# Sliding-window attention and an ELU layer on one core: other ways to build the constants, and loads of q, k, v cut in halves

## The chip, the core and the metric

The kernel runs on one core of a Trainium2 chip. A core has five engines that run their own instruction streams and wait for each other by semaphores: TensorE (PE in the profile; PEld is its weight load), VectorE (DVE), ScalarE (ACT), GpSimd (POOL) and SyncE (SP, which here only issues transfers). Data lie in an on-chip memory of 128 partitions; PE writes into accumulation banks (PSUM). Transfers are run by 16 DMA engines and are issued here from SP or from POOL. The metric is the device time of one execution in microseconds (us), lower is better; the time of a kernel is the median over its runs.

## What is computed

Attention over 8 batches and 8 heads, 576 positions of 64 values, with a causal window of 128 and a linear bias by distance, and then a layer with ELU on the result. Cut to what matters:

```python
scores = q @ k^T / sqrt(64)
rel = pos[:, None] - pos[None, :]
slopes = 2.0 ** (-8.0 * (arange(8) + 1) / 8)
scores = where((rel >= 0) & (rel < 128), scores - slopes * abs(rel), -1e9)
attn = softmax(scores) @ v                        # 8 x 8 x 576 x 64
x = attn.transpose(0, 2, 1, 3).reshape(4608, 512)
h = x @ w_in                                      # 512 -> 2048
out = where(h > 0, h, exp(min(h, 0)) - 1) @ w_out # 2048 -> 512
```

All inputs and the output are float32; the kernel works in float16 with float32 accumulation.

## The kernel before

**One list of slots.** Work is put into numbered slots by `at(slot, function, ...)` (L541); the loop at the end (L655) walks the slots and emits, in each: scores, one group of 16 or 8 `hidden` matmuls, `elu` of the group before, the attention work, then everything else in the order in which it was registered, and one group of `output` matmuls. The order within each engine is therefore the order written here; only semaphores move work in time. A slot takes about 2.1 us once all parts run. From the first `hidden` groups one reads where slots lie: slot 4 at 18.7 us, 8 at 25.0, 9 at 26.5, 10 at 28.2, 11 at 29.9, 13 at 33.9, 14 at 36.4, 18 at 46.1, 21 at 53.9, 25 at 68.4.

**Attention.** Each batch has 16 score groups (`BANKS`), one per slot, that start at slot 16b + 5 for batch b from 1 on. `scores` (L350) multiplies 32-position-ordered blocks of k and q out of `QK[b % 2]`, a tile of 128 partitions x 5 blocks x (q, k) x 8 heads x 128. Partitions 0 to 63 hold the transposed q and k. For batch 0 only these are used, and the bias comes from a second matmul with `DM` and `cI` (L378). From batch 1 on the partitions from 64 on carry constants, so that one matmul gives scores, bias and part of the mask: 32 rows of group flags (64 to 95; `g_`) and in 96 to 127 (`r_`) two rows for the bias, the others being zero. ACT takes the exponential (`EX`, L382), DVE cuts it with `band` (`cut`, L390), PE multiplies with v (`values`, L404), DVE normalizes into `xn` (L424, L425), and `turn` brings it as columns into `xT`: by PE for batches 0 and 1, by a transposing DMA on SP (L433) from batch 2 on.

**The layer.** `hidden` (L452): PE into `hp` (three banks), ACT exponential `e` (L465), POOL clamps `e` (L466). `elu`: DVE makes `g` from `e` and `hp` (L473), which also frees the bank. `output` (L492) follows some 10 slots later. From group 40 on there are four slots between the `turn` that completes 256 columns of `xT` and the `hidden` that reads them.

**Inputs.** q and k go by POOL-issued DMAs, with a cast, into `stq[b]` (512 positions, `load_qk`, L78) and `stt[b]` (the last 64, `load_tail`), v into `vs[b]` (`load_v4`) and its tail straight into `VP[b % 2]`. Each of these tiles has two buffers. DVE transposes q and k in 32x32 blocks into `tt` (`squares`, L327) and SP copies them into `QK` (`collect`, L333), eight of each per batch; batch 1 goes through PE (`transposes`). `place_v` (L116) moves 32 partitions of v at a time into `VP`, mostly on POOL: 16 pieces per batch. For batches 3 to 7 the code loads b + 2 during batch b: k at s0 + 10, q at s0 + 13, v at s0 + 15, tails at s0 + 26 and + 27, v's tail at s0 + 19, and v's pieces two per slot from s0 + 20 to s0 + 27, where s0 = 16b + 5.

**Constants.** `posi`, an int32 iota of positions (L154), is written on POOL in the preamble. `groups`, `flags`, `terms` and `group_rows` (L227 to L259) work it into `TQ` and `TK` on DVE in slots 9 to 13; `fill_q` (ACT) and `fill_k` (POOL) spread these over the heads into `QK[1]` in slots 14 to 26, `k_term` (DVE, eight times, slots 14 to 19) writes the bias rows, one per head, and `fill_other` (SP, slots 21 to 28) copies the 64 constant partitions of `QK[1]` to `QK[0]`, block by block. `last_blocks` (DVE, slot 12) makes the last 128 columns of `DM`, `bands` makes `band` from it, and `zeros` (DVE, slot 4) clears padding.

Of the kernel before, what the change touches and what calls it, by code (L numbers as in the profile page):

```python
# [19 lines left out]
def kernel(  # L20
# [33 lines left out]
    def one(shape, dt, name):  # L54
        return const.tile(shape, dt, name=name, tag=name)
# [47 lines left out]
        nc.gpsimd.dma_start(  # L103
            stt[b][:, w, :, :], (q, k)[w][b, :, 512:576, :].rearrange("h s d -> s h d"))

    def load_v4(b):

        vs[b] = stage.tile([128, H, 4, D], F16, name="vs", tag="vs", bufs=2)
        nc.gpsimd.dma_start(vs[b].rearrange("p h j d -> p h (j d)"),
                            v[b, :, 0:512, :].rearrange("h (p j) d -> p h (j d)", j=4))  # L110

    def load_v4_tail(b):
        nc.gpsimd.dma_start(VP[b % 2][0:64, 4, :, 0:D],
# [24 lines left out]
    with tc.manual_schedule():  # L138

        row = one([128, 1], I32, "row")  # L140
        col = one([128, 128], I32, "col")
        posi = one([128, 576], I32, "posi")
        load_half(0, 1, 0, 0, 4)
        load_half(0, 0, 0, 0, 4)
        nc.gpsimd.iota(row, pattern=[[0, 1]], base=0, channel_multiplier=1)
# [5 lines left out]
        load_half(0, 1, 1)  # L151
        load_half(0, 0, 1)
        load_v_half(0, 1)
        nc.gpsimd.iota(posi[:, 0:512].rearrange("p (n j i) -> p n j i", j=4, i=32),  # L154
                       pattern=[[128, 4], [1, 4], [4, 32]], base=0, channel_multiplier=0)
        nc.gpsimd.iota(posi[:, 512:576], pattern=[[1, 64]], base=512, channel_multiplier=0)

        def small(name, dt=F32):
            return one([128, 1], dt, name)
# [16 lines left out]
        def seen(c, t, key, off, n):  # L176

            V.tensor_scalar(out=nd[:, c:c + n], in0=t, scalar1=key, scalar2=-1.0,
                            op0=ALU.subtract, op1=ALU.mult)
            if off:  # L180
                V.tensor_scalar(out=nd[:, c:c + n], in0=nd[:, c:c + n], scalar1=float(-off),
                                scalar2=None, op0=ALU.add)
# [15 lines left out]
        unseen(128, 128, -127.0, ALU.is_lt)  # L198
        join(0, 256)

        def last_blocks():
            seen(256, posi[:, 512:576], kpos, -384, 64)
            seen(320, posi[:, 512:576], rowf, -512, 64)
            unseen(256, 64, -127.0, ALU.is_lt)
            unseen(320, 64, 0.0, ALU.is_gt)
            join(256, 128)

        def bands():
            V.tensor_scalar(out=band, in0=DM, scalar1=-1000.0, scalar2=BIG, op0=ALU.is_gt, op1=ALU.mult)

        def zeros():
            for i in range(2):
                V.memset(QK[i][0:64 + 64 * i, 4, 1, :, 64:128], 0.0)
                V.memset(VP[i][64:128, 4, :, 0:D], 0.0)
            for e in EX:
                V.memset(e[:, 512:576], 0.0)


        g_, r_ = slice(64, 96), slice(96, 128)
        gof = small("gof")  # L220
        is96, is97, isx = small("is96"), small("is97"), small("isx")
        TQ = one([128, 640], F16, "TQ")
        TK = one([128, 640], F16, "TK")
        gi = one([128, 320], I32, "gi")
        pm = one([128, 576], F32, "pm")

        def groups():  # L227
            V.tensor_scalar(out=gof, in0=rowf, scalar1=-8.0, scalar2=1024.0, op0=ALU.mult, op1=ALU.add)
            V.tensor_scalar(out=gi[g_, 0:256], in0=posi[g_, 0:256], scalar1=gof[g_, :], scalar2=None,
                            op0=ALU.add)  # L230
            V.tensor_scalar(out=gi[g_, 256:320], in0=posi[g_, 512:576], scalar1=gof[g_, :],
                            scalar2=None, op0=ALU.add)
            V.tensor_scalar(out=gi[g_, :], in0=gi[g_, :], scalar1=255, scalar2=None,
                            op0=ALU.bitwise_and)

        def flags():
            V.tensor_scalar(out=is96, in0=rowf, scalar1=96.0, scalar2=None, op0=ALU.is_equal)
            V.tensor_scalar(out=is97, in0=rowf, scalar1=97.0, scalar2=None, op0=ALU.is_equal)
            V.tensor_scalar(out=isx, in0=is97, scalar1=-1.0, scalar2=None, op0=ALU.mult)

        def terms():

            flags()
            V.tensor_scalar(out=pm[r_, :], in0=posi[r_, :], scalar1=float(-MID), scalar2=None, op0=ALU.add)
            V.tensor_scalar(out=TQ[r_, 0:576], in0=pm[r_, :], scalar1=isx[r_, :], scalar2=is96[r_, :],
                            op0=ALU.mult, op1=ALU.add)
            V.tensor_scalar(out=TK[r_, 0:576], in0=pm[r_, :], scalar1=is96[r_, :],
                            scalar2=is97[r_, :], op0=ALU.mult, op1=ALU.add)
            for t in (TQ, TK):
                nc.gpsimd.memset(t[64:128, 576:640], 0.0)  # L250

        def group_rows():
            for d0, s0, n in ((0, 0, 256), (512, 256, 64)):
                V.tensor_scalar(out=TQ[g_, d0:d0 + n], in0=gi[g_, s0:s0 + n], scalar1=134.5,
                                scalar2=-30000.0, op0=ALU.is_gt, op1=ALU.mult)
                V.tensor_scalar(out=TK[g_, d0:d0 + n], in0=gi[g_, s0:s0 + n], scalar1=7.5,
                                scalar2=None, op0=ALU.is_lt)
            for t in (TQ, TK):
                V.tensor_copy(t[g_, 256:512], t[g_, 0:256])  # L259

        def fill_q(n):
            nc.scalar.copy(QK[1][64:128, n, 0, :, :],
                           TQ[64:128, 128 * n:128 * n + 128].unsqueeze(1).broadcast_to([64, H, 128]))

        def fill_k(n):
            nc.gpsimd.tensor_scalar(  # L266
                out=QK[1][g_, n, 1, :, :], in0=TK[g_, 128 * n:128 * n + 128].unsqueeze(1)
                .broadcast_to([32, H, 128]), scalar1=1.0, scalar2=0.0, op0=ALU.mult, op1=ALU.add)

        def k_term(h):  # L270
            V.tensor_scalar(out=QK[1][r_, :, 1, h, :], in0=TK[r_, :].rearrange("p (n c) -> p n c", c=128),
                            scalar1=8.0 * 2.0 ** (-8.0 * (h + 1) / H), scalar2=None, op0=ALU.mult)

        def fill_other(n):
            nc.sync.dma_start(QK[0][64:128, n].rearrange("p w h c -> p (w h c)"),
                              QK[1][64:128, n].rearrange("p w h c -> p (w h c)"))

# [70 lines left out]
        def scores(b, s):  # L350
            i, p = BANKS[s]
            t = ps_s.tile([128, 512], F32, name="sp", tag="sps")
            qk = QK[b % 2]

            r = 64 if b == 0 else 128

            def mm(o, h, kc, qc, n):
                nc.tensor.matmul(t[:, o:o + n], qk[0:r, kc, 1, h, :], qk[0:r, qc, 0, h, 0:n],  # L358
                                 start=b > 0 or o == 0, stop=b > 0)

            if i == 0:
                hs = [4 * p + l for l in range(4)]
                for l in range(4):
                    mm(128 * l, hs[l], 0, 0, 128)
            elif i < 4:
                hs = [2 * p, 2 * p + 1]
                for l in range(2):
                    mm(256 * l, hs[l], i, i, 128)
                    mm(256 * l + 128, hs[l], i - 1, i, 128)
            else:  # L370
                hs = [4 * p + l for l in range(4)]
                for l in range(4):
                    mm(128 * l, hs[l], 3, 4, 64)
                    mm(128 * l + 64, hs[l], 4, 4, 64)
            if b == 0:
                c, n = columns(i)
                for l, h in enumerate(hs):
                    nc.tensor.matmul(t[:, n * l:n * l + n], cI[:, h, :], DM[:, c:c + n],  # L378
                                     start=False, stop=l == len(hs) - 1)
            e = ex[b, s] = EX[count[0] % 4]  # L380
            count[0] += 1
            nc.scalar.activation(e[:, 0:512], t, AF.Exp, scale=0.125)  # L382
# [189 lines left out]
        for b in range(B):  # L572
# [25 lines left out]
                    at(s0 + (6 + n if b > 1 else 8 + n if n < 4 else 9 + n), collect, b + 1, n)  # L598
                at(s0 + (24 if b else 31), transposes_tail, b + 1)
            if b + 2 < B and b:  # L600
                for i, w in enumerate((1, 0)):
                    at(s0 + 10 + 3 * i, load_qk, b + 2, w)
                    at(s0 + 26 + i, load_tail, b + 2, w)
                at(s0 + 15, load_v4, b + 2)
                at(s0 + 19, load_v4_tail, b + 2)
                for n in range(4):
                    for u in range(2):
                        at(s0 + 20 + 2 * n + u, place_v, b + 2, n, (2 * u, 2 * u + 1), nc.gpsimd)


        at(6, place_v, 0, 2, (0, 1), nc.gpsimd)
        at(7, place_v, 0, 2, (2,), nc.gpsimd)
        at(7, place_v, 0, 2, (3,), nc.scalar)
        for u in range(2):
            at(10 + u, place_v, 0, 3, (2 * u, 2 * u + 1), nc.gpsimd)
        at(3, load_wi, 3)
        at(5, load_wo, 0, 1)
        at(8, load_wo, 1, 1)
        at(9, load_wo, 2, 1)
        at(10, load_wo, 3, 1)  # L620
        at(4, zeros)
        at(9, groups)
        at(10, terms)
        at(12, last_blocks)
        at(13, group_rows)
        at(14, bands)
        for n, m in enumerate((14, 16, 18, 23, 26)):
            at(m, fill_q, n)
            at(m, fill_k, n)
        for h in range(H):  # L630
            at(14 + 3 * h // 4, k_term, h)
        for n in range(5):
            at((21, 22, 23, 25, 28)[n], fill_other, n)
        for i, w in enumerate((1, 0)):
# [69 lines left out]
```

## Time and profile before

| | |
|---|---|
| median of 11 runs | 352.06 us (349.36 to 354.47) |
| the profiled execution | 351.41 us |
| its span | 349.6 us |
| granted PE clock, mean | 0.99 |
| busy: PE, DVE, POOL, ACT | 327.9, 249.5, 212.7, 208.0 us |
| DMA issued by POOL (q, k, v, weights) | 18.35 MB |
| DMA issued by SP and others (output, collect, transposes, copies) | 20.46 MB |
| landing: full load of q, k or v, 512 KB | 8.1 to 8.9 us, median |
| landing: collect, QK<-tt, 128 KB | 2.4 us |
| landing: transpose, xT<-xn | 3.6 us |
| landing: fill_other, QK<-QK, 256 KB | 2.9 us |

The span is the part of the execution between the first and last instruction; 1.8 us lie around it. Busy time of an engine is the time in its instructions, and PE's is modelled, so that a full PE is not a PE at its peak. In the lines of a timeline the columns are start, duration, engine, source line, operation, result and operand with their shapes, number of instructions merged, and in brackets the idle time in front and what ended it. Transfers are listed with their time from issue to landing.

### The profile page before, as it was taken

What the parts mean: (1) busy time and instruction counts of PE and PEld (TensorE: products, weight loads), DVE (VectorE), ACT (ScalarE), POOL (GpSimd) and SP (SyncE); (2) the same over time, 40 slices, a digit from 0 to 9 for tenths busy, and PEclk for the clock granted to TensorE, in tenths of its full rate; (3) what the DMA queues carried; (4) which work ended last, traced back from release to release, by engine and by line L of the source; (5) the groups of instructions that cost most, each with busy time, mean ns of one, the idle gap of its engine ahead of it and who ended that gap; (6) DMA issues with size and microseconds to landing.
All of it is one profiled execution on the core that took longest, in us unless ns stands there. A gap on an engine that the chain in (4) does not pass through costs nothing.

```text
span 349.6 us, 9328 instructions
## 1 busy us (share of the span) xinstructions
PE 327.9 (94%) x3604; PEld 242.7 (69%) x3604; DVE 249.5 (71%) x572; ACT 208.0 (59%) x360; POOL 212.7 (61%) x325
## 2 busy tenths in 40 slices
PE   5899996798999969999999999999999999999995
PEld 4678674577777747877777777777777777666663
DVE  4468986888779678958994999498967676533330
ACT  5566658676885636665666666666566656344431
POOL 8538994454788945896589568957972223333330
PEclk9699999999999999999999999999999999999999
DMA  7998999647893797569947974896462222311122
GB/s 90 179 203 119 184 177 181 125 84 123 126 169 79 110 191 107 98 105 194 122 107 120 191 106 99 141 193 93 104 108 54 55 47 52 68 35 30 32 60 61
DMA packets 66428, 39.54 MB, mean 113 GB/s; under 512 B 31120, under 2 KB 60048, under 8 KB 66384
## 3 DMA queue, kind: packets, MB, share of 16 engines
q0 software_dynamic: 41936, 18.35, 44.5%
q1 hardware_dynamic: 24272, 20.46, 26.4%
q8 instruction: 28, 0.46, 0.6%
q14 instruction: 16, 0.13, 0.1%
q10 hardware_dynamic: 176, 0.13, 0.1%
HBM read 36.70 MB, written 9.44 MB: 132 GB/s over the span
## 4 chain that ended last, share of the span: by engine, by line
PE 74%; POOL 8%; DVE 6%; DMA 5%; ACT 3%; issue 2%; SPq 1%; POOLq 0%; ACTq 0%; DVEq 0%
PE hp L461 30%; PE op L504 29%; PE sp L358 7%; PE av L404 4%; DMA xT<-xn 3%; POOL VP L121 3%; POOL e L466 2%; DMA QK<-tt 2%; PE spare L536 2%; DVE g L473 1%; ACT EX L382 1%; PE sp L378 1%; DVE QK L296 1%; DVE xn L425 1%; POOL QK L266 1%
## 5 line engine op out<-in xcount | busy, mean ns | idle before, releaser
L466 POOL TENSOR_SCALAR e<-e 128x512 f32<-128x512 f32 x144 | 90.4, 629 | 116.4 <-ACT e L465 101.6
L461 PE MATMUL hp<-xT,wi 128*128 128x256 f16 (+3 forms) x1536 | 150.2, 246 | 3.3 <-DMA xT<-xn 1.7
L473 DVE SCALAR_TENSOR_TENSOR g<-e,hp 128x512 f16<-128x512 f32 x144 | 98.0, 681 | 66.8 <-POOL e L466 65.8
L504 PE MATMUL op<-wo,g 128*128 128x512 f16 x560 | 143.1, 379 | 0.0
L461 PEld LDWEIGHTS <-wi 128*128 128x128 f16 x1536 | 117.8, 98 | 17.8 <-issue 3.7
L465 ACT ACTIVATE e<-hp 128x512 f32<-128x512 f32 x144 | 86.1, 598 | 48.2 <-PE hp L461 47.1
L382 ACT ACTIVATE EX<-sp 128x512 f16<-128x512 f32 x128 | 76.5, 598 | 63.1 <-PE sp L358 52.5
L121 POOL TENSOR_SCALAR VP<-vs 32x512 f16<-32x512 f16 x105 | 69.1, 659 | 8.1 <-DMA vs<-in_v_dram 1.1
L504 PEld LDWEIGHTS <-g 128*128 128x128 f16 x560 | 47.1, 97 | 34.3
L358 PEld LDWEIGHTS <-QK 128*128 128x128 f16 (+1 forms) x576 | 39.1, 98 | 30.5 <-issue 3.7
L390 DVE TENSOR_TENSOR EX<-EX,band 128x512 f16<-128x512 f16 x112 | 54.8, 489 | 4.8 <-ACT EX L382 4.1
L358 PE MATMUL sp<-QK 128*128 128x128 f16 (+3 forms) x576 | 50.3, 215 | 3.0 <-ACT EX L382 1.4
L404 PE MATMUL av<-VP,EX 128*128 128x65 f16 x576 | 38.8, 194 | 4.8 <-DVE EX L390 1.9
L404 PEld LDWEIGHTS <-EX 128*128 128x128 f16 x576 | 32.1, 98 | 7.9 <-DVE EX L390 2.4
L425 DVE TENSOR_TENSOR xn<-av,rden 128x256 f16<-128x256 f32 x80 | 34.0, 425 | 2.8
L327 DVE STREAM_TRANSPOSE tt<-stq 128x512 f16<-128x512 f16 x48 | 33.6, 701 | 1.5 <-DMA QK<-tt 1.5
L508 ACT COPY ob<-op 128x512 f32<-128x512 f32 x35 | 20.5, 587 | 15.6 <-PE op L504 15.1
L424 DVE RECIPROCAL rden<-av 128x4 f32<-128x4 f32 x80 | 14.0, 176 | 5.9 <-PE av L404 5.7
L536 PE MATMUL spare<-ident 128*128 128x128 f16 x84 | 9.0, 277 | 3.8 <-DVE kmod L169 3.8
L125 ACT COPY VP<-vs 32x512 f16<-32x512 f16 x17 | 10.5, 615 | 0.4
L536 PEld LDWEIGHTS <-ident 128*128 128x128 f16 x84 | 7.2, 128 | 4.0 <-DVE kmod L169 3.8
L346 DVE COPY QK<-tpt 64x512 f16<-64x512 f16 x16 | 6.7, 418 | 0.5 <-PE tpt L341 0.4
(85 smaller groups left out, 146.3 us busy)
## 6 DMA issues: line engine op xcount, KB each, us to landing
out_dram<-ob SPq DMA_DIRECT2D x126, 64.0 KB, 1.9
QK<-tt SPq DMA_DIRECT2D x48, 128.0 KB, 2.4
stq<-in_k_dram POOLq DMA_DIRECT2D x7, 512.0 KB, 8.1
stq<-in_q_dram POOLq DMA_DIRECT2D x7, 512.0 KB, 8.3
vs<-in_v_dram POOLq DMA_DIRECT2D x7, 512.0 KB, 8.9
wi<-in_moe_w_in_dram POOLq DMA_DIRECT2D x4, 512.0 KB, 9.8
wo<-in_moe_w_out_dram POOLq DMA_DIRECT2D x4, 512.0 KB, 7.4
QK<-QK SPq DMA_DIRECT2D x5, 256.0 KB, 2.9
```

Source lines behind the costliest of these rows:

```text
L121: engine.tensor_scalar(out=o, in0=i, scalar1=1.0, scalar2=0.0, op0=ALU.mult, op1=ALU.add)
L327: V.transpose(out=tt[b][:, dh, w, hs, :, :].rearrange("p h j i -> p (h j) i"), in_=stq[b][:, w, hs, :, 32 * dh:32 * dh + 32].rearrange("p ...
L358: nc.tensor.matmul(t[:, o:o + n], qk[0:r, kc, 1, h, :], qk[0:r, qc, 0, h, 0:n], start=b > 0 or o == 0, stop=b > 0)
L382: nc.scalar.activation(e[:, 0:512], t, AF.Exp, scale=0.125)
L390: V.tensor_tensor(out=e, in0=e, in1=band[:, c:c + n].unsqueeze(1).broadcast_to([128, 512 // n, n]), op=ALU.min)
L404: nc.tensor.matmul(a[:, l, :], e[:, c:c + 128], vp[:, n, h, 0:D + 1], start=st, stop=sp)
L425: V.tensor_tensor(out=xnt[b, i][:, 4 * half:4 * half + 4, :], in0=a[:, :, 0:D], in1=r.unsqueeze(2).broadcast_to([128, 4, D]), op=ALU.mult)
L461: nc.tensor.matmul(p[:, l * w + u0:l * w + u1], w_in_sb[:, c, fc * 128:(fc + 1) * 128], xT[:, c, x0:x0 + u1 - u0], start=(c == 0), stop=(c ...
L465: nc.scalar.activation(e, p, AF.Exp)
L466: nc.gpsimd.tensor_scalar(out=e, in0=e, scalar1=1.0, scalar2=0.0, op0=ALU.min, op1=ALU.max)
L473: V.scalar_tensor_tensor(out=gs[t][:, f0:f0 + nf, c0:c0 + w], in0=sh(es.pop((t, j))), scalar=1.0, in1=sh(hps.pop((t, j))), op0=ALU.subtrac ...
L504: nc.tensor.matmul(ops[t], gs[t][:, fc, ts * 128:(ts + 1) * 128], w_out_sb[:, fc, :], start=(fc == 0), stop=(fc == NFC - 1))
```

## The change

The constants are built by other means. Two rows of positions (`kterm` on eight partitions, `qterm` on one) come from iotas on POOL as float32 and float16; the slopes by head come from an iota over the exponent bits; ones, and the slopes as rows, from memsets on DVE (`tables`). One DVE operation makes the eight bias rows (`terms`). Ten small DMAs on SP (`spread`, slot 11) put them into partitions 96 and 97 of `QK[1]` and 97 of `TQ`; `k_term`, `flags` and `group_rows` are gone. The group flags come from an iota that already counts groups. The constants now end at partition 97: `scores` uses 98 rows, and `fill_q` and `fill_other` handle 34 partitions. `last_blocks` uses an iota and a copy of columns that `DM` already has. `zeros` has one memset more.

The loads of q, k and v of batches 3 to 7 are each cut in two by heads (0 to 3 and 4 to 7). With o = s0 + 2, + 4 and + 1 for b = 1, b = 2 and b from 3 on, the k halves are at o and o + 2, q at o + 4 and o + 6, v at o + 8 and o + 10, the tails at o + 12 and o + 14; v's tail stays. v's pieces are placed one per slot from s0 + 18 to s0 + 33. Of batch 0's fourth v block, the pieces that were in slots 10 and 11 are in 9 and 10, and one goes to DVE.

```diff
@@ -103,11 +103,12 @@
         nc.gpsimd.dma_start(
             stt[b][:, w, :, :], (q, k)[w][b, :, 512:576, :].rearrange("h s d -> s h d"))
 
-    def load_v4(b):
-
-        vs[b] = stage.tile([128, H, 4, D], F16, name="vs", tag="vs", bufs=2)
-        nc.gpsimd.dma_start(vs[b].rearrange("p h j d -> p h (j d)"),
-                            v[b, :, 0:512, :].rearrange("h (p j) d -> p h (j d)", j=4))
+    def load_v4(b, h0=0, h1=H):
+
+        if b not in vs:
+            vs[b] = stage.tile([128, H, 4, D], F16, name="vs", tag="vs", bufs=2)
+        nc.gpsimd.dma_start(vs[b][:, h0:h1, :, :].rearrange("p h j d -> p h (j d)"),
+                            v[b, h0:h1, 0:512, :].rearrange("h (p j) d -> p h (j d)", j=4))
 
     def load_v4_tail(b):
         nc.gpsimd.dma_start(VP[b % 2][0:64, 4, :, 0:D],
@@ -139,7 +140,11 @@
 
         row = one([128, 1], I32, "row")
         col = one([128, 128], I32, "col")
-        posi = one([128, 576], I32, "posi")
+
+        gi = one([128, 320], I32, "gi")
+        slope = one([H, 1], I32, "slope")
+        kterm = one([H, 640], F32, "kterm")
+        qterm = one([1, 640], F16, "qterm")
         load_half(0, 1, 0, 0, 4)
         load_half(0, 0, 0, 0, 4)
         nc.gpsimd.iota(row, pattern=[[0, 1]], base=0, channel_multiplier=1)
@@ -151,9 +156,10 @@
         load_half(0, 1, 1)
         load_half(0, 0, 1)
         load_v_half(0, 1)
-        nc.gpsimd.iota(posi[:, 0:512].rearrange("p (n j i) -> p n j i", j=4, i=32),
-                       pattern=[[128, 4], [1, 4], [4, 32]], base=0, channel_multiplier=0)
-        nc.gpsimd.iota(posi[:, 512:576], pattern=[[1, 64]], base=512, channel_multiplier=0)
+        nc.gpsimd.iota(gi[64:96, 0:256].rearrange("p (n j i o) -> p n j i o", j=4, i=16, o=2),
+                       pattern=[[16, 2], [0, 4], [1, 16], [0, 2]], base=0, channel_multiplier=-1)
+        nc.gpsimd.iota(gi[64:96, 256:320].rearrange("p (i o) -> p i o", o=8),
+                       pattern=[[1, 8], [0, 8]], base=0, channel_multiplier=-1)
 
         def small(name, dt=F32):
             return one([128, 1], dt, name)
@@ -198,82 +204,89 @@
         unseen(128, 128, -127.0, ALU.is_lt)
         join(0, 256)
 
+        nl = one([128, 64], F32, "nl")
+
         def last_blocks():
-            seen(256, posi[:, 512:576], kpos, -384, 64)
-            seen(320, posi[:, 512:576], rowf, -512, 64)
-            unseen(256, 64, -127.0, ALU.is_lt)
-            unseen(320, 64, 0.0, ALU.is_gt)
-            join(256, 128)
+            V.tensor_copy(DM[:, 256:320].rearrange("p (i j) -> p i j", j=4),
+                          DM[:, 128:256].rearrange("p (j i) -> p i j", i=32)[:, 0:16, :])
+            V.tensor_scalar(out=nm[:, 320:384], in0=nl, scalar1=0.0, scalar2=-BIG,
+                            op0=ALU.is_gt, op1=ALU.mult)
+            V.tensor_tensor(out=DM[:, 320:384], in0=nl, in1=nm[:, 320:384], op=ALU.add)
 
         def bands():
             V.tensor_scalar(out=band, in0=DM, scalar1=-1000.0, scalar2=BIG, op0=ALU.is_gt, op1=ALU.mult)
 
         def zeros():
+            P = V
             for i in range(2):
-                V.memset(QK[i][0:64 + 64 * i, 4, 1, :, 64:128], 0.0)
-                V.memset(VP[i][64:128, 4, :, 0:D], 0.0)
+                P.memset(QK[i][0:64 + 64 * i, 4, 1, :, 64:128], 0.0)
+                P.memset(VP[i][64:128, 4, :, 0:D], 0.0)
+            P.memset(QK[1][64:128, 4, 0, :, 64:128], 0.0)
             for e in EX:
-                V.memset(e[:, 512:576], 0.0)
-
-
-        g_, r_ = slice(64, 96), slice(96, 128)
-        gof = small("gof")
-        is96, is97, isx = small("is96"), small("is97"), small("isx")
+                P.memset(e[:, 512:576], 0.0)
+
+        g_ = slice(64, 96)
         TQ = one([128, 640], F16, "TQ")
-        TK = one([128, 640], F16, "TK")
-        gi = one([128, 320], I32, "gi")
-        pm = one([128, 576], F32, "pm")
+        TG = one([128, 320], F16, "TG")
+        TK = one([H, 640], F16, "TK")
+        slopes = one([1, H, 128], F16, "slopes")
+
+        nc.gpsimd.iota(slope, pattern=[[0, 1]], base=129 << 23, channel_multiplier=-(1 << 23))
+
+        def iota_rows(t, m):
+
+            nc.gpsimd.iota(t[:, 0:512].rearrange("p (n j i) -> p n j i", j=4, i=32),
+                           pattern=[[128 * m, 4], [m, 4], [4 * m, 32]], base=-MID * m,
+                           channel_multiplier=0, allow_small_or_imprecise_dtypes=True)
+            nc.gpsimd.iota(t[:, 512:576], pattern=[[m, 64]], base=(512 - MID) * m,
+                           channel_multiplier=0, allow_small_or_imprecise_dtypes=True)
+
+        def iota_last():
+            nc.gpsimd.iota(nl, pattern=[[-1, 64]], base=0, channel_multiplier=1,
+                           allow_small_or_imprecise_dtypes=True)
+
+        def tables():
+            for t in (kterm, qterm):
+                V.memset(t[:, 576:640], 0.0)
+            V.memset(TQ[96:98, :], 1.0)
+            for h in range(H):
+                V.memset(slopes[:, h, :], 8.0 * 2.0 ** (-8.0 * (h + 1) / H))
+
+
+        def terms():
+            V.tensor_scalar(out=TK, in0=kterm, scalar1=slope.bitcast(F32), scalar2=None, op0=ALU.mult)
+
+        def spread():
+
+            nc.sync.dma_start(TQ[97:98, :], qterm)
+            nc.sync.dma_start(QK[1][97:98, :, 1, :, :].rearrange("p n h c -> p n (h c)"),
+                              slopes.rearrange("p h c -> p (h c)").unsqueeze(1).broadcast_to([1, 5, H * 128]))
+            for h in range(H):
+                nc.sync.dma_start(QK[1][96:97, :, 1, h, :],
+                                  TK[h:h + 1, :].rearrange("p (n c) -> p n c", c=128))
 
         def groups():
-            V.tensor_scalar(out=gof, in0=rowf, scalar1=-8.0, scalar2=1024.0, op0=ALU.mult, op1=ALU.add)
-            V.tensor_scalar(out=gi[g_, 0:256], in0=posi[g_, 0:256], scalar1=gof[g_, :], scalar2=None,
-                            op0=ALU.add)
-            V.tensor_scalar(out=gi[g_, 256:320], in0=posi[g_, 512:576], scalar1=gof[g_, :],
-                            scalar2=None, op0=ALU.add)
-            V.tensor_scalar(out=gi[g_, :], in0=gi[g_, :], scalar1=255, scalar2=None,
-                            op0=ALU.bitwise_and)
-
-        def flags():
-            V.tensor_scalar(out=is96, in0=rowf, scalar1=96.0, scalar2=None, op0=ALU.is_equal)
-            V.tensor_scalar(out=is97, in0=rowf, scalar1=97.0, scalar2=None, op0=ALU.is_equal)
-            V.tensor_scalar(out=isx, in0=is97, scalar1=-1.0, scalar2=None, op0=ALU.mult)
-
-        def terms():
-
-            flags()
-            V.tensor_scalar(out=pm[r_, :], in0=posi[r_, :], scalar1=float(-MID), scalar2=None, op0=ALU.add)
-            V.tensor_scalar(out=TQ[r_, 0:576], in0=pm[r_, :], scalar1=isx[r_, :], scalar2=is96[r_, :],
-                            op0=ALU.mult, op1=ALU.add)
-            V.tensor_scalar(out=TK[r_, 0:576], in0=pm[r_, :], scalar1=is96[r_, :],
-                            scalar2=is97[r_, :], op0=ALU.mult, op1=ALU.add)
-            for t in (TQ, TK):
-                nc.gpsimd.memset(t[64:128, 576:640], 0.0)
-
-        def group_rows():
+            V.tensor_scalar(out=gi[g_, :], in0=gi[g_, :], scalar1=31, scalar2=None, op0=ALU.bitwise_and)
             for d0, s0, n in ((0, 0, 256), (512, 256, 64)):
-                V.tensor_scalar(out=TQ[g_, d0:d0 + n], in0=gi[g_, s0:s0 + n], scalar1=134.5,
+                V.tensor_scalar(out=TQ[g_, d0:d0 + n], in0=gi[g_, s0:s0 + n], scalar1=16.5,
                                 scalar2=-30000.0, op0=ALU.is_gt, op1=ALU.mult)
-                V.tensor_scalar(out=TK[g_, d0:d0 + n], in0=gi[g_, s0:s0 + n], scalar1=7.5,
-                                scalar2=None, op0=ALU.is_lt)
-            for t in (TQ, TK):
-                V.tensor_copy(t[g_, 256:512], t[g_, 0:256])
+            V.tensor_copy(TQ[g_, 256:512], TQ[g_, 0:256])
+            V.tensor_scalar(out=TG[g_, :], in0=gi[g_, :], scalar1=0.0, scalar2=None, op0=ALU.is_equal)
 
         def fill_q(n):
-            nc.scalar.copy(QK[1][64:128, n, 0, :, :],
-                           TQ[64:128, 128 * n:128 * n + 128].unsqueeze(1).broadcast_to([64, H, 128]))
+            c, w = 128 * n, 128 if n < 4 else 64
+            nc.scalar.copy(QK[1][64:98, n, 0, :, 0:w],
+                           TQ[64:98, c:c + w].unsqueeze(1).broadcast_to([34, H, w]))
 
         def fill_k(n):
+            c, w = (128 * (n % 2), 128) if n < 4 else (256, 64)
             nc.gpsimd.tensor_scalar(
-                out=QK[1][g_, n, 1, :, :], in0=TK[g_, 128 * n:128 * n + 128].unsqueeze(1)
-                .broadcast_to([32, H, 128]), scalar1=1.0, scalar2=0.0, op0=ALU.mult, op1=ALU.add)
-
-        def k_term(h):
-            V.tensor_scalar(out=QK[1][r_, :, 1, h, :], in0=TK[r_, :].rearrange("p (n c) -> p n c", c=128),
-                            scalar1=8.0 * 2.0 ** (-8.0 * (h + 1) / H), scalar2=None, op0=ALU.mult)
+                out=QK[1][g_, n, 1, :, 0:w], in0=TG[g_, c:c + w].unsqueeze(1)
+                .broadcast_to([32, H, w]), scalar1=1.0, scalar2=0.0, op0=ALU.mult, op1=ALU.add)
 
         def fill_other(n):
-            nc.sync.dma_start(QK[0][64:128, n].rearrange("p w h c -> p (w h c)"),
-                              QK[1][64:128, n].rearrange("p w h c -> p (w h c)"))
+            nc.sync.dma_start(QK[0][64:98, n].rearrange("p w h c -> p (w h c)"),
+                              QK[1][64:98, n].rearrange("p w h c -> p (w h c)"))
 
 
 
@@ -352,7 +365,7 @@
             t = ps_s.tile([128, 512], F32, name="sp", tag="sps")
             qk = QK[b % 2]
 
-            r = 64 if b == 0 else 128
+            r = 64 if b == 0 else 98
 
             def mm(o, h, kc, qc, n):
                 nc.tensor.matmul(t[:, o:o + n], qk[0:r, kc, 1, h, :], qk[0:r, qc, 0, h, 0:n],
@@ -598,37 +611,42 @@
                     at(s0 + (6 + n if b > 1 else 8 + n if n < 4 else 9 + n), collect, b + 1, n)
                 at(s0 + (24 if b else 31), transposes_tail, b + 1)
             if b + 2 < B and b:
-                for i, w in enumerate((1, 0)):
-                    at(s0 + 10 + 3 * i, load_qk, b + 2, w)
-                    at(s0 + 26 + i, load_tail, b + 2, w)
-                at(s0 + 15, load_v4, b + 2)
+                o = s0 + (1, 2, 4, 1)[min(b, 3)]
+                for n in range(2):
+                    at(o + 2 * n, load_qk, b + 2, 1, 4 * n, 4 * n + 4)
+                    at(o + 2 * n + 4, load_qk, b + 2, 0, 4 * n, 4 * n + 4)
+                    at(o + 2 * n + 8, load_v4, b + 2, 4 * n, 4 * n + 4)
+                    at(o + 2 * n + 12, load_tail, b + 2, 1 - n)
                 at(s0 + 19, load_v4_tail, b + 2)
                 for n in range(4):
-                    for u in range(2):
-                        at(s0 + 20 + 2 * n + u, place_v, b + 2, n, (2 * u, 2 * u + 1), nc.gpsimd)
+                    for j in range(4):
+                        at(s0 + 18 + 4 * n + j, place_v, b + 2, n, (j,), nc.gpsimd)
 
 
         at(6, place_v, 0, 2, (0, 1), nc.gpsimd)
         at(7, place_v, 0, 2, (2,), nc.gpsimd)
         at(7, place_v, 0, 2, (3,), nc.scalar)
-        for u in range(2):
-            at(10 + u, place_v, 0, 3, (2 * u, 2 * u + 1), nc.gpsimd)
+        at(9, place_v, 0, 3, (0, 1), nc.gpsimd)
+        at(10, place_v, 0, 3, (2,), nc.gpsimd)
+        at(10, place_v, 0, 3, (3,), V)
         at(3, load_wi, 3)
         at(5, load_wo, 0, 1)
         at(8, load_wo, 1, 1)
         at(9, load_wo, 2, 1)
         at(10, load_wo, 3, 1)
         at(4, zeros)
+        at(8, tables)
+        at(3, iota_rows, kterm, 1)
+        at(5, iota_rows, qterm, -1)
+        at(5, iota_last)
         at(9, groups)
         at(10, terms)
+        at(11, spread)
         at(12, last_blocks)
-        at(13, group_rows)
         at(14, bands)
         for n, m in enumerate((14, 16, 18, 23, 26)):
             at(m, fill_q, n)
             at(m, fill_k, n)
-        for h in range(H):
-            at(14 + 3 * h // 4, k_term, h)
         for n in range(5):
             at((21, 22, 23, 25, 28)[n], fill_other, n)
         for i, w in enumerate((1, 0)):
```

## The prediction

> **What bounds the kernel now.** First the page's part two, the span in 40 slices of 8.74 us, for PE, POOL and DMA:
>
> ```profile
> PE   5899996798999969999999999999999999999995
> POOL 8538994454788945896589568957972223333330
> DMA  7998999647893797569947974896462222311122
> ```
>
> PE is full from the 16th slice to the last. What it loses lies in front of that: slices 4 to 9 and slice 15. The busy time by stage puts amounts on it (columns: length; PE, PEld, DVE, ACT, POOL busy with counts; clock, DMA share, GB/s):
>
> ```profile
> 30.00:40.00 10.00, 8.96 (x134) 7.30 (x132) 9.51 (x27) 5.78 (x9) 9.28 (x15) 1.00 1.22 180
> 40.00:50.00 10.00, 9.07 (x105) 6.21 (x102) 9.42 (x22) 6.19 (x10) 9.48 (x12) 1.00 1.49 176
> 50.00:60.00 10.00, 7.71 (x102) 5.51 (x100) 6.94 (x14) 7.48 (x11) 5.68 (x9) 1.00 1.33 189
> 60.00:70.00 10.00, 7.58 (x103) 5.68 (x103) 7.77 (x21) 7.24 (x12) 4.20 (x6) 1.00 0.71 124
> 120.00:130.00 10.00, 6.52 (x70) 4.53 (x67) 6.42 (x16) 3.65 (x7) 5.88 (x9) 1.00 1.28 176
> ```
>
> Idle PE: 1.04 + 0.93 + 2.29 + 2.42 + 3.48 us; with 0.48 (20 to 30), 1.31 (80 to 90) and 0.36 (150 to 170) it is 12.3 us, the ceiling of any gain after the start-up. From 170 to 330 us the same table has PE at 20.00 of 20.00. From 30 to 50 us DVE and POOL are both above 92%; from 50 to 70 neither is.
>
> The timeline of PE names the stalls that this change can reach:
>
> ```profile
> 33.94 1.05 PE L461 MATMUL hp<-xT,wi 128*128 128x128 f16 x16 [0.58 <-DVE g L473]
> 35.44 0.28 PE L404 MATMUL av<-VP,EX 128*128 128x65 f16 x4 [0.46 <-POOL VP L121]
> ...
> 124.13 0.29 PE L404 MATMUL av<-VP,EX 128*128 128x65 f16 x4 [1.47 <-DVE EX L390]
> ...
> 127.21 1.03 PE L461 MATMUL hp<-xT,wi 128*128 128x256 f16 x8 [1.70 <-DMA xT<-xn]
> ```
>
> What stands behind the last two is in POOL's timeline:
>
> ```profile
> 116.60 1.36 POOL L121 TENSOR_SCALAR VP<-vs 32x512 f16<-32x512 f16 x2
> 118.02 0.93 POOL L82 DMA_DIRECT2D stq<-in_k_dram  x1
> 119.03 0.60 POOL L466 TENSOR_SCALAR e<-e 128x512 f32<-128x512 f32 x1
> 119.59 0.70 POOL L103 DMA_DIRECT2D stt<-in_q_dram  x1
> 120.37 1.48 POOL L121 TENSOR_SCALAR VP<-vs 32x512 f16<-32x512 f16 x2
> 121.93 1.19 POOL L466 TENSOR_SCALAR e<-e 128x512 f32<-128x512 f32 x2
> 123.06 0.94 POOL L82 DMA_DIRECT2D stq<-in_q_dram  x1
> ```
>
> Two v blocks, two loads and a tail stand between the e's, so e falls behind; DVE's g waits for it (1.88 us before 122.58), the EX behind g comes late, and PE idles 1.47 (0.31 before, at 120.41). Meanwhile the k load goes out at 118.02 and q at 123.06, into the transpose xT<-xn issued at 118.07, which takes 9.10 us in the chain of waits against a median of 3.6: PE idles 1.70 more.
>
> **Constants, DVE.** Removed, from the timeline: groups 1.40 us (28.08 to 29.48), flags and terms 2.49 (30.67 to 33.16), last_blocks 2.02, group_rows 2.07, and eight k_term of 0.48 = 3.85: 11.8 us. Added: one more memset in zeros (0.27, with its gap 0.36); tables, eleven memsets, by the nearest rows 0.05 (EX, four in 0.20) to 0.14 (VP, two in 0.27) each, taken at 0.1, so 1.1; new groups 0.32 + 0.77 + 0.17 + 0.21 + about 0.5 = 2.0; terms as one 8x640, by the 32x576 row 0.75; last_blocks three 128x64 of 0.2; one v block of 0.33. Sum 5.1, net 6.7 us less, nearly all between 30 and 50 us. The zeros memset is on the path: DVE runs without a gap from 20.5 to 25.9 and PE's wait at 24.43 is for it, so 0.36 is lost. The tables sit in DVE's 1.53 us of idle before 27.48; with that cover gone they cost 1.1.
>
> **Constants, POOL.** Gone: two memsets (33.41 less 32.95 = 0.46) and one v block (0.65). New: two pairs of iotas, by the posi rows 0.66 + 0.23 each, and one of 0.23. The first pair falls into 5.71 us of idle before 20.54, the rest (1.12) into 2.92 before 26.83; uncovered, 2.0. The v block gone from slot 11 ends the 0.46 at 35.44.
>
> From 28.3 to 51.8 POOL has no gap over about half a us, and e, the v blocks, fill_k and the loads all pass it in order. So the early gain has two bounds: POOL's own saving, 1.11 less the 0.36 of later start = 0.75; and all the PE waits for DVE or POOL in that stretch, 0.58 + 0.46 + 0.29 + 0.60 + 0.41 + 0.66 less 0.36 = 2.6. I take **1.4**, nearer to POOL's, whose chain doesn't break. ACT's copies between 54 and 62 us stay, and with them the 1.36 and 1.51 us of PE wait there.
>
> **Constants, SP.** spread adds ten DMAs: at 0.56 us each (the QK<-QK issue) 5.6 us of SP, which has nothing to do until 46.95. They are wanted by fill_q(0) on ACT (39.00; queued behind it EX and e) and by the scores of batch 1 (58.76); terms is done about 32, the last lands before 41. fill_q(0) needs only the first, which waits for tables alone. Nothing on the path; uncovered, ACT is 2 us late.
>
> **The copy to QK0, on 34 partitions.** Here a rule speaks against the change. By the row, 64 partitions land in 2.9 us. The Trainium skill, "DMA: Bandwidth & Descriptors", section on why a DMA increments its semaphore by 16, says that a DMA runs on the largest number of engines up to 16 that divides the slowest dimension: 64 gives 16, 34 gives 2. No run here shows a count other than multiples of 16. By the row's pace alone 34 partitions would take under 2.9. By the rule, 17 rows of 4 KB follow each other on each of two engines: at (2.9 - 1.9) / 4 = 0.25 us a row (1.9 is the landing of the 64 KB output), 17 x 0.25 + 1.9 = 6.2 us, an estimate. I believe the rule, and still cost it at nothing: copies 1 to 4, issued 61.8 to 74.3, bring 68 rows, 17 us, done by about 83 with the loads' share; batch 2's scores want QK0 at 92.89.
>
> **98 rows in the scores.** The timeline has four 64-row scores matmuls from 30.97 to the next group at 31.30, 0.33 us, four 128-row ones from 68.20 to 68.42, 0.22, and the entry into the 64-row form shows the same 0.1. "TensorEngine Tiling (Array Packing)", key properties, says that switching the tiling mode drains the array, and lists no row tile between 64 and 128. So 98 rows stay in the full mode: 0. Were they a mode of their own, 0.21 x 112 groups = 23.5 us.
>
> **Loads in halves.** POOL pays 15 more issues. A quarter load on 64 partitions takes 0.63, a full one 0.92; I take 0.75 a half, 1.5 a pair, so 15 x 0.58 = 8.7 us over the run. By slot of 2.1 us: e 0.70, one v block 0.68, half a load 0.38, sum 1.76; before, two blocks and e filled 2.1, with loads and tails on top. The cover is 0.3 us a slot; without it the 8.7 us would show. Batch 3's loads move from slots 31 to 36 to slots 23 to 33, where POOL is idle over half of the time.
>
> At 116 to 128 us a slot now has one block, and every second one half a load: the POOL backlog goes (0.31 + 1.47), and the transpose meets at most one half with four slots (8.4 us) until its use. It should land in 4 to 5 us, so the 1.70 goes as well. Of 3.48 I take **3.3**; of the 0.36 near 157, the same pile-up, **0.2**. PE is full behind that.
>
> **Sum.** 351.41 - 1.4 - 3.3 - 0.2 = 346.5 for the profiled execution (span 349.6 and 1.8 around it). The median is 0.65 above it: **347.2 us** is predicted.
>
> **Rivals.** (a) The early saving reaches its bound of 2.6 and DVE's earlier copies shorten the ACT stretch by up to 1: 345. For it: ACT idles 2.05 behind DVE's QK copy at 54.01. Against: POOL.
> (b) The crowding is only moved: half loads now stand beside every transpose and collect, the 1.70 stays or returns elsewhere, and POOL's chain eats the early part: only the 1.8 of backlog is won, 350.3, with no measurable change above it. For it: DMA share is already 1.0 to 1.5 in many stages.
> (c) Slower: the two engines jam. In the crowded stretch the copy at 50.90 took 7.2 us, (7.2 - 1.9) / 4 = 1.3 us a row. The collects for batch 2 queue behind the 68 rows, and 92.89 - 61.8 = 31 us allow 0.46 us a row: that is where it decides. At 0.6 the rows end at 102.6, 9.7 us late: 357. Against: DMA share is 0.71 and 0.37 from 60 to 80; for it: batch 3's loads move into that stretch.
> (d) 98 rows drain the array: 347.2 + 23.5 = 371.
>
> **How the numbers follow.** Chances: forecast 0.62 (own range 345.3 to 349), (a) 0.11, (b) 0.11, (c) 0.13, (d) 0.03. About 0.5%, 1.8 us, is what a measurement here tells from no change, so faster is below 350.3: 0.62 + 0.11 + 0.03 of (b) = 0.76; same 0.08; slower 0.16. The range 344.8 to 352.5 leaves out (c), (d) and a sliver below.
>
> **What would show it.** PE without waits over 0.5 us at 33 to 46 and at 116 to 130; xT<-xn landing at most 6 us; QK<-QK near 6 us (rule right) or under 3 (wrong); four 98-row scores in 0.22; e never more than a slot behind ACT's. A PE wait for QK<-tt near 90 us would be (c), and a transpose still at 9 us would be (b). Any new wait after 130 us proves the sum wrong.

## The result and the profile after

The changed kernel takes **347.29 us** (median of 12 runs, 343.51 to 350.55) against 352.01 for the kernel before beside it: ratio 0.9844, 95% interval 0.9815 to 0.9872. Predicted were 347.2 us and a range of 344.8 to 352.5. The profiled execution took 347.44 us, with a span of 345.7. Medians here are over all executions of a kernel and ratios over the fast ones alone, within 1.5% of its fastest; the profiles of placement alone (355.29 us) and of 98 rows alone (352.70 us) are of slow ones.

The page's part two, for the same engines as before (40 slices of 8.64 us):

```profile
PE   5999996798999999999999999999999999999995
POOL 8647994566599889887877787766555222333330
DMA  7997999559667999996899498934442212211122
```

The weak slice of PE at 122 to 131 us is gone; slices 7 and 8, at 52 to 69 us, are as weak as they were. POOL no longer comes in bursts: between 95 and 240 us it is 60% busy or more in every slice. The stages, in the columns of the table before:

```profile
30.00:40.00 10.00, 9.09 (x131) 7.19 (x127) 9.18 (x22) 6.56 (x11) 9.35 (x14) 1.00 1.13 166
40.00:50.00 10.00, 10.00 (x129) 7.64 (x127) 5.57 (x10) 6.12 (x9) 9.13 (x13) 1.00 1.60 198
50.00:60.00 10.00, 6.97 (x91) 4.89 (x89) 6.19 (x12) 7.81 (x11) 5.42 (x8) 1.00 1.30 182
60.00:70.00 10.00, 7.92 (x104) 5.81 (x104) 8.20 (x22) 7.12 (x13) 5.04 (x7) 1.00 0.52 90
120.00:130.00 10.00, 10.00 (x108) 7.24 (x106) 7.45 (x21) 6.18 (x11) 8.93 (x13) 1.00 1.06 163
```

From 40 to 50 us DVE fell from 9.42 to 5.57 us and PE is full; at 120 to 130 PE has 10.00 in place of 6.52. POOL's timeline there shows one block per e, and half a load for every second:

```profile
117.14 0.60 POOL L479 TENSOR_SCALAR e<-e 128x512 f32<-128x512 f32 x1
117.82 0.61 POOL L122 TENSOR_SCALAR VP<-vs 32x512 f16<-32x512 f16 x1
118.52 0.76 POOL L479 TENSOR_SCALAR e<-e 128x512 f32<-128x512 f32 x1
119.35 0.61 POOL L122 TENSOR_SCALAR VP<-vs 32x512 f16<-32x512 f16 x1
120.02 0.78 POOL L110 DMA_DIRECT2D vs<-in_v_dram  x1
120.88 0.60 POOL L479 TENSOR_SCALAR e<-e 128x512 f32<-128x512 f32 x1
```

But the timeline of PE has one wait behind 130 us that was not there before:

```profile
156.82 1.03 PE L474 MATMUL hp<-xT,wi 128*128 128x256 f16 x8 [0.52 <-DMA xT<-xn]
```

**A measure that leaves the start-up out.** Of the profiled executions told of here the first hidden group's exponential on ACT starts anywhere from 16.84 to 20.69 us, also in kernels whose start-up is the same, so spans say little. The table takes the start of ACT's exponential of hidden group 4 as zero (groups counted from 0), and gives for later groups the difference to the profile of before, in us; below zero is earlier. The kernels other than the changed one are those of the experiments below.

| kernel | group 12 | group 16 | group 36 | group 40 | group 60 | last |
|---|---|---|---|---|---|---|
| changed | -1.55 | -0.98 | -1.24 | -5.19 | -4.95 | -4.73 |
| changed, a second profile | -1.55 | -0.99 | -1.28 | -5.23 | -5.08 | -4.86 |
| constants alone | -1.54 | -1.07 | -0.85 | -1.64 | -1.61 | -1.31 |
| loads and placement alone | +1.18 | +2.58 | +2.22 | -1.75 | +0.16 | +0.16 |
| placement alone | +1.10 | +2.22 | +2.95 | +2.27 | +4.61 | +4.60 |
| 98 rows alone | +1.18 | +0.73 | +0.57 | -0.49 | -0.45 | +0.19 |
| changed, undivided loads | -1.55 | -1.08 | -1.74 | -5.69 | -6.13 | -5.92 |
| changed, two blocks a slot | -1.54 | -0.98 | -0.27 | -1.84 | -0.91 | +0.53 |

Groups 4 to 16 lie at 31 to 70 us, 36 to 40 at 116 to 128. The new kernel repeats to 0.13 us. The old constants do not: three further profiles of them lose 1.10 to 1.18 us more between groups 4 and 12 than the profile of before, which was a lucky one there. Rows with old constants are therefore to be read against +1.18 at group 12 and, by the 98 rows, +0.73 at group 16.

### The profile page after: what moved, and what is told of

It reads as the page before. It is cut to its first block, busy times and chain, and to the rows that moved or that the text cites. A ratio compares the mean times of both kernels' runs of the same rounds, so it can differ in the third digit from the quotient of the medians.

```text
span 345.7 us, 9392 instructions
## 1 busy us (share of the span) xinstructions
PE 328.6 (95%) x3604; PEld 243.5 (70%) x3604; DVE 243.6 (70%) x563; ACT 207.9 (60%) x360; POOL 220.1 (64%) x343
## 4 chain that ended last, share of the span: by engine, by line
PE 79%; DVE 8%; POOL 4%; ACT 3%; DMA 3%; issue 2%; SPq 0%; POOLq 0%; ACTq 0%; DVEq 0%
PE hp L474 31%; PE op L517 31%; PE sp L371 7%; PE av L417 4%; DVE g L486 2%; DMA xT<-xn 2%; PE spare L549 2%; POOL e L479 1%; DVE xn L438 1%; DVE EX L403 1%; DVE tt L340 1%; PE sp L391 1%; ACT EX L395 1%; DVE QK L309 1%; ACT e L478 1%
## 5 line engine op out<-in xcount | busy, mean ns | idle before, releaser
L122 POOL TENSOR_SCALAR VP<-vs 32x512 f16<-32x512 f16 x104 | 65.7, 632 | 9.9 <-DMA vs<-in_v_dram 2.1
L371 PEld LDWEIGHTS <-QK 98*128 98x128 f16 (+1 forms) x576 | 39.3, 98 | 30.5 <-issue 4.1
L403 DVE TENSOR_TENSOR EX<-EX,band 128x512 f16<-128x512 f16 x112 | 51.5, 460 | 3.9 <-ACT EX L395 3.4
L371 PE MATMUL sp<-QK 98*128 98x128 f16 (+3 forms) x576 | 50.7, 215 | 2.8 <-ACT EX L395 1.4
L82 POOL DMA_DIRECT2D stq<-in_k_dram x12 | 9.8, 819 | 0.4 <-issue 0.2
```

Of the source, the lines that this page charges most:

```text
L122: engine.tensor_scalar(out=o, in0=i, scalar1=1.0, scalar2=0.0, op0=ALU.mult, op1=ALU.add)
L403: V.tensor_tensor(out=e, in0=e, in1=band[:, c:c + n].unsqueeze(1).broadcast_to([128, 512 // n, n]), op=ALU.min)
```

## Experiments

**Which half gives what.** Constants alone (the change without its two hunks on loads and placement), and the loads alone:

```diff
-                for i, w in enumerate((1, 0)):
-                    at(s0 + 10 + 3 * i, load_qk, b + 2, w)
...
+                o = s0 + (1, 2, 4, 1)[min(b, 3)]
+                for n in range(2):
+                    at(o + 2 * n, load_qk, b + 2, 1, 4 * n, 4 * n + 4)
...
```

> The kernel changed, with loads and placement of v of batches 3 to 7 as before: the constants alone. Theory (POOL's chain bounds the early part): 0.4 to 1.4 us below before, ratio 0.997, and the wait of 1.7 us for the transposing DMA near 127 stays. Rival (the stretch at 50 to 62 us is bound by ACT and takes the gain back): 0 to 0.3 us.

Measured: 350.08 us against 351.79, ratio 0.9932 (0.9894 to 0.9970), 1.7 us less. Both waits at 120 to 127 us are still there:

```profile
123.03 0.29 PE L416 MATMUL av<-VP,EX 128*128 128x65 f16 x4 [1.47 <-DVE EX L402]
125.62 1.05 PE L473 MATMUL hp<-xT,wi 128*128 128x256 f16 x8 [1.21 <-DMA xT<-xn]
```

The gain is real, a little above the stated 0.4 to 1.4, and the rival that ACT gives it all back is out. Some is given back: against 98 rows alone, a profile with the old constants, 2.7 us are won by group 12 and 1.8 are left at group 16.

> The kernel before with the loads of batches 3 to 7 in halves and v placed one block per slot, constants as before. Theory (two separate gains; the waits of 0.31, 1.47 and 1.70 us at 120 to 127 us belong to the loads): 3.3 to 3.9 us below before, ratio 0.990, the waits of PE at 120 to 127 gone, those at 33 to 46 unchanged. Rival (the constants feed the later part, because POOL and DVE arrive there less late): under 2 us below before.

Measured: 349.01 us, ratio 0.9919 (0.9882 to 0.9955), 2.8 us less, under the 3.3 to 3.9 that the theory gave. From group 36 to 40 it wins 3.97 us, as the theory says. Then it loses 1.9 by group 60, at one place. First PE; then the transpose that it waits for, on SP, and the second half of v, on POOL:

```profile
158.92 1.03 PE L462 MATMUL hp<-xT,wi 128*128 128x256 f16 x8 [2.27 <-DMA xT<-xn]
```

```profile
149.93 1.24 SPq L434 DMA_TRANSPOSE xT<-xn  x1
```

```profile
149.93 0.79 POOL L110 DMA_DIRECT2D vs<-in_v_dram  x1
```

Both are issued at 149.93; the transpose needs 8.9 us to land, the half load 8.4. The changed kernel's 0.52 us at 156.82 is the same meeting (149.27 and 149.28). In the table this profile ends at +0.16 although its median is lower than before's: it carries the usual old constants (1.18 by group 12) and 1.9 us at half PE clock (last section). By the medians the two parts add up: 1.7 + 2.8 = 4.5 us, against 4.7.

**Placement alone.** One block per slot from s0 + 20 on, loads as before:

```diff
-                    for u in range(2):
-                        at(s0 + 20 + 2 * n + u, place_v, b + 2, n, (2 * u, 2 * u + 1), nc.gpsimd)
+                    for j in range(4):
+                        at(s0 + 20 + 4 * n + j, place_v, b + 2, n, (j,), nc.gpsimd)
```

> The kernel before with only v of batches 3 to 7 placed one block per slot from s0 + 20 on, all loads as before. Theory (a pile-up on POOL of two v blocks, loads and tails in one slot makes e late): the 0.31 and 1.47 us at 120 to 124 go, the 1.70 for the transposing DMA stays, since the full loads of k and q still follow each other: 1.5 to 2 us below before. Rival (the loads alone are at fault): no change.

Measured: 352.84 us, ratio 0.9990 (0.9944 to 1.0035): nothing won. In its one profile the waits of 0.31 and 1.47 do go, but the transpose costs PE 2.64 us instead of 1.70, and a wait for g of 1.52 appears at 164.85. Spread over twice the slots, the blocks meet the full loads of the next batch instead: POOL has six of them with three full loads and a tail between 154 and 165 us.

**The other way round: early half loads, but two blocks per slot as before.**

> The kernel changed, with v of batches 3 to 7 placed as before, two blocks per slot from s0 + 20 to s0 + 27. Theory (it is the loads that no longer fall among the pairs of blocks; either of the two parts removes the pile-up): within 1 us of the kernel changed. Rival (two blocks a slot fill POOL, and a half load on top makes e late): 1 to 3 us slower than the kernel changed, PE waits for g at 116 to 130 us.

Measured: 353.01 us, ratio 1.0023 (0.9993 to 1.0054). Here the theory fell and the rival holds, and by more than it said. From 116 us on PE waits for g five times, 3.5 us in all, first here:

```profile
119.18 1.03 PE L474 MATMUL hp<-xT,wi 128*128 128x256 f16 x8 [1.67 <-DVE g L486]
```

Two blocks and e fill POOL's slot, and every half load on top puts e behind. So neither part pays without the other: with the early loads, placing one block per slot is worth 5.7 us (353.01 against 347.29, from two sittings; 5.3 in the table).

**Is the halving needed?** Undivided loads at the slots of the first halves, run in two sittings:

```diff
-                for n in range(2):
-                    at(o + 2 * n, load_qk, b + 2, 1, 4 * n, 4 * n + 4)
-                    at(o + 2 * n + 4, load_qk, b + 2, 0, 4 * n, 4 * n + 4)
-                    at(o + 2 * n + 8, load_v4, b + 2, 4 * n, 4 * n + 4)
+                at(o, load_qk, b + 2, 1)
+                at(o + 4, load_qk, b + 2, 0)
+                at(o + 8, load_v4, b + 2)
```

> The kernel changed, with the loads of k, q and v of batches 3 to 7 undivided, at the slots of the first halves (four slots apart). Theory (it is the spacing that keeps the transposing DMA short, not the halving): within 0.7 us of the kernel changed, transposes landing in at most 7 us. Rival (a transpose queues behind a whole 512 KB load): waits of PE for the transposing DMA come back, 1 to 3 us above the kernel changed.

> The kernel changed itself, beside the next three on the same chip. Expected: 347.3 us, ratio to before 0.984 to 0.987.

> The kernel changed with undivided loads at the slots of the first halves, once more and with more runs. Theory (the second half of v is issued together with the transpose of the third block and lengthens it; the undivided load is through by then): 0.5 to 2 us below the kernel changed, no PE wait for the transposing DMA. Rival (the first result was a lucky start): equal within 0.5 us.

Measured: 345.49 us, ratio 0.9795 (0.9746 to 0.9845), and in the second sitting 344.57 us, 0.9793 (0.9741 to 0.9844), where the changed kernel beside it had 347.23 us, 0.9860 (0.9803 to 0.9918). The intervals overlap, but both sittings and two profiles agree: 1.2 us less in the table, 1.8 and 2.7 us by the medians, and so better than the "within 0.7 us" of the first theory. No PE wait for a transpose is left. The undivided v, issued at

```profile
143.35 0.92 POOL L110 DMA_DIRECT2D vs<-in_v_dram  x1
```

is four us ahead of the transpose (147.45), where the second half came together with it. The theory had the load landed by then; it landed at 150.41, three us after the transpose's issue. And the transpose is only part of the 1.2: half of it is there by group 24 (-1.52 against -0.95), with a wait of 0.42 us for EX that the changed kernel has at 82.90 and this one has not; what removed that was not looked for. Of the change, the halving is the part that costs; its spacing pays.

**What bounds 30 to 62 us?** On the undivided loads, first fill_k moved from POOL to DVE, and then batch 1's pieces of v from ACT to DVE as well:

```diff
-            nc.gpsimd.tensor_scalar(
-                out=QK[1][g_, n, 1, :, 0:w], ...
+            V.tensor_copy(QK[1][g_, n, 1, :, 0:w], ...
...
-                    at(18 + 2 * n + u, place_v, 1, n, (2 * u + 1,), nc.scalar)
+                    at(18 + 2 * n + u, place_v, 1, n, (2 * u + 1,), V)
```

> Undivided early loads, and the five fill_k copies on DVE instead of POOL, which takes 3.1 us off POOL between 39 and 50 us. Theory (POOL's chain of work bounds the stretch from 30 to 52 us): 0.7 to 2 us below undivided early loads, hidden group 16 at least 0.7 us earlier relative to group 4. Rival (ACT's copies from 50 to 62 us bound it): no change.

> As the one before, and the six pieces of batch 1's v that ACT places in slots 20 to 25 (0.62 each) go to DVE. Theory (ACT bounds 54 to 62 us): 1 to 2.5 us below the one before, the PE wait of 1.36 us for EX near 60 us shorter. Rival (DVE's chain of EX, reciprocal and xn bounds it): no change or up to 1 us slower.

Measured: fill_k on DVE 344.73 us, ratio 0.9770 (0.9704 to 0.9835); both 343.97 us, 0.9773 (0.9713 to 0.9834); neither is told apart from 344.57. In the profiles group 12 stands at -1.55 and -1.54, just where it stood (-1.55): with two fill_k less on POOL by then, PE gains nothing up to 48 us. POOL did not bound that stretch once the constants were changed. After 48 us it did: with fill_k moved, group 14 stands at -2.42 against -1.09, 1.33 us earlier, and these two waits of the undivided loads (second profile) are gone:

```profile
47.92 0.61 PE L329 MATMUL tp<-ident,stq 128*128 128x128 f16 x8 [0.37 <-ACT QK L321]
49.84 0.40 PE L371 MATMUL sp<-QK 64*128 64x64 f16 x8 [0.45 <-DVE QK L359]
```

At 59.28 us the PE clock of this profile then fell to half (last section), and at group 16 nothing is left of the 1.33 (-0.94), so how much of it would last is open. With ACT's pieces moved as well, group 14 comes another 0.64 us earlier (-3.06), and group 16 stands 1.30 us ahead of the undivided loads (-2.38 against -1.08). The wait for EX near 60 us, for the undivided loads and for both moves:

```profile
59.37 0.38 PE L371 MATMUL sp<-QK 98*128 98x128 f16 x4 [1.36 <-ACT EX L395]
```

```profile
55.01 0.38 PE L370 MATMUL sp<-QK 98*128 98x128 f16 x4 [0.73 <-ACT EX L394]
```

So POOL and ACT both hold up parts of 48 to 62 us; how the 1.30 is divided between the two moves is not shown, and the medians don't resolve it.

**98 rows.** The kernel before with `r = 64 if b == 0 else 98`:

> The kernel before with 98 rows instead of 128 in the scores of batches 1 to 7, nothing else. Theory (98 rows stay in the full mode of the array): no change, four scores matmuls still 0.22 us before the next group. Rival (a mode of its own, drained at each entry and exit): 23 us slower.

Its four executions, 352.67 us in the median beside 351.44, gave no interval; a loss of 23 us is out. The spacing settles the mechanism:

```profile
69.84 0.39 PE L358 MATMUL sp<-QK 98*128 98x128 f16 x4
70.06 1.06 PE L461 MATMUL hp<-xT,wi 128*128 128x128 f16 x16
```

Four matmuls in 0.22 us, as with 128 rows.

**34 partitions.** All five copies to QK0 moved to slot 33, whole or cut into 32 and 2 partitions:

```diff
-            at((21, 22, 23, 25, 28)[n], fill_other, n)
+            at(33, fill_other, n)
```

> The kernel changed, with all five copies of the constants to QK0 in slot 33, so late that batch 2's scores in slot 37 and the collects in slots 34 to 37 meet them. Theory (34 partitions run on two DMA engines, 85 rows of 4 KB one after another on each pair, 0.2 to 0.25 us each per engine): the copies take 17 to 21 us and PE waits 5 to 12 us for QK near 95 us. Rival (16 engines): under 1 us slower.

> As the one before, each copy cut into the 32 partitions of the flags and the 2 of the bias. Theory (32 partitions run on 16 engines, 2 on two, one row each): the PE wait of the one before is gone but for 1 to 2 us, although five more transfers are issued. Rival (the wait comes from the lateness alone): the same wait as the one before.

Measured: 359.94 us (two executions), ratio 1.0272 (1.0189 to 1.0355), and 347.19 us, 0.9901 (0.9855 to 0.9948). PE at the first scores of batch 2, whole and cut:

```profile
101.45 0.61 PE L371 MATMUL sp<-QK 98*128 98x128 f16 x4 [11.73 <-DMA QK<-tt]
```

```profile
91.42 0.40 PE L372 MATMUL sp<-QK 98*128 98x128 f16 x4 [1.97 <-DMA QK<-tt]
```

The wait names the collects, which stand behind the copies. The same bytes, cut between 32 and 2 partitions, are a matter of 9.8 us of wait. The rival, lateness, explains at most the 1.97 that is left. The rest bears out what the Trainium skill, "DMA: Bandwidth & Descriptors", section on why a DMA increments its semaphore by 16, says of dividing the slowest dimension: 32 gives 16 engines, 34 gives 2. The engines themselves were not seen; of the first copy's rows, at most 3 are under way at a time in the changed kernel's packets, and up to 12 with 64 partitions in the kernel before.

## Why the prediction was right, and where it was not

- **The pile-up at 116 to 128 us** was taken at 3.3; groups 36 to 40 win 3.95. The mechanism held, and loads and placement alone win 3.97 there. Other profiles of the old loads lose 0.66 to 2.64 us to that transpose in place of 1.70, so the size is that of one execution.
- **The constants** were taken at 1.4. Against the profile of before they give 0.98 between groups 4 and 16; against the usual run of the old constants more (1.7, with the 0.73 of 98 rows alone), and 1.7 by medians. The step that failed is "nearer to POOL's, whose chain doesn't break": in the changed kernel, taking work off POOL moved nothing up to 48 us, so the size came out close for a wrong reason. The profile of before had it: between 30 and 50 us DVE waits for POOL's e twice, 0.38 us in all, so DVE and not POOL set the pace; after the change it waits five times, 4.91 us. The longest of each:

```profile
49.01 0.69 DVE L473 SCALAR_TENSOR_TENSOR g<-e,hp 128x512 f16<-128x512 f32 x1 [0.21 <-POOL e L466]
47.16 0.69 DVE L486 SCALAR_TENSOR_TENSOR g<-e,hp 128x512 f16<-128x512 f32 x1 [2.06 <-POOL e L479]
```

  What went were DVE's late g's: PE waits for them 0.87 us there before, 2.4 to 2.5 in the three other profiles of the old constants, and 0.33 in the changed kernel. The longest with the old constants (98 rows alone), and the one that is left:

```profile
43.07 1.05 PE L461 MATMUL hp<-xT,wi 128*128 128x128 f16 x16 [1.15 <-DVE g L473]
34.43 1.05 PE L474 MATMUL hp<-xT,wi 128*128 128x128 f16 x16 [0.33 <-DVE g L486]
```

  The 0.46 for VP, which is POOL's, went as forecast; none of the other three profiles has it. The wait for xn stayed (0.60, now 0.58 at 36.30, over the 0.5 that the signs allow).
- **DVE's items** were mis-sized one by one. The tables were put at 1.1 in an idle of 1.53 and ran from 26.65 to 28.79, 2.1 us, which delayed g; last_blocks is about 1.5, not 0.6. The sum still fell. The zeros memset did cost: group 4 is 0.27 later after group 0 (11.45 against 11.18), against 0.36.
- **The half load's issue** was put at 0.75 and takes 0.78 to 0.80, hidden as said. What was missed is not on POOL: the sentence that the transpose "meets at most one half" and lands in 4 to 5 us. It can take 8.9 beside one half, with collects and outputs in flight; in the changed kernel PE, waiting for it, goes on 7.5 us after its issue. That is the new wait after 130 us, 0.4 to 0.5 us in two profiles and 2.27 in one. The 0.36 near 157 did go, and this came in its place: in this the sum was wrong, and undivided loads get it back.
- **The narrow copy** was costed at nothing for its slack, rightly: PE has no wait for QK<-tt near 90 us. The trace has no landing of this copy; rows of the first follow each other over 3.7 us in its packets, 0.22 us for each of 17, against 0.25. What rival (c) describes does happen once the copies are late, and costs 12.7 us there.
- **98 rows** cost nothing, as said; (a)'s point that ACT's stretch can be shortened is borne out, though not by this change.
- **The total** is in part luck. Of 4.9 us (1.4 + 3.3 + 0.2), the table has 4.73, as 1.24 to group 36, 3.95 to group 40, and 0.46 lost after that: an excess in one term covers the loss in another.

## What to carry to other kernels

When an in-order engine both computes and issues loads, count its slot with everything in it: here early loads or single blocks alone won nothing or little, and together 2.8 us. Cutting a load in two makes two issues of one, and here one of them fell together with a short transfer that has a deadline; the whole load, issued four us ahead of that transfer, was better. And before relying on a stall's size, look at more than one profile of the same work.

## What the runs showed of the hardware

A PE that idles through the waits at 54 to 60 us is sometimes put on half clock for 3.41 us. Loads and placement alone, by stage (clock in the third column from the end):

```profile
58.00:60.00 2.00, 1.03 (x12) 1.03 (x12) 0.43 (x1) 1.92 (x4) 0.00 (x0) 0.79 0.80 105
60.00:62.00 2.00, 2.00 (x21) 1.63 (x19) 0.82 (x3) 0.87 (x3) 0.07 (x1) 0.50 0.59 140
62.00:64.00 2.00, 1.58 (x19) 0.88 (x17) 1.47 (x4) 1.10 (x3) 1.53 (x3) 0.85 0.94 193
```

Sixteen hidden matmuls took 1.70 us there from first to next, not 0.89. It struck three of the profiles (loads alone, placement alone, fill_k on DVE) and spared the others with the same waits, and cost 1.5 to 1.9 us between groups 14 and 16, where profiles without it move by 0.1 or less (98 rows alone, undivided loads). With the 11.73 us wait, which ended at 101.45, the clock was halved for 13.65 us (93.28 to 106.94), after the 1.97 us wait and in placement alone after 2.64 us for 3.41 us each; after the 2.27 us of loads alone and the 1.70 us of the kernel before it stayed full. So a stall can cost more than its length, in some executions and not in others; what decides it was not tried.
